# A new written order for the opening of a fused attention and routing kernel

## The chip, the cores and the metric

The kernel runs on one core of one Trainium2 chip. Its time is the device time of one execution in microseconds. Six executions of the kernel before gave a median of 715.14 us (713.99 to 716.82).

## What is computed

Duo attention feeds a mixture of experts whose routing is Sinkhorn-balanced. There are 4 batches, 8 heads, 768 positions and 64 values per head; heads with `is_retrieval` see all earlier positions, the others see the first 4 positions and the last 64.

```python
scores = q @ k.T / sqrt(64);  scores = where(mask, scores, -1e9)
a = exp(scores - max);  a /= a.sum(-1);  x = a @ v       # x: 3072 tokens x 512
logits = x @ w_gate;  P = exp(logits - logits.max())     # 8 experts
for _ in range(8):
    P /= P.sum(1, keepdims=True);  P /= P.sum(0, keepdims=True);  P *= N / E
out = sum over e of P[:, e:e+1] * (relu(x @ w1[e]) @ w2[e])   # 512 -> 1024 -> 512
```

## The kernel before

**Units, rounds and tasks.** Attention is cut into 24 units `(b, g, u)`: batch, a block of 256 queries, and half of the heads (two pairs `a` of two heads). For block `g` a pair has `g + 1` chunks of keys; each pair and chunk is a task, and two tasks make a round, of which there are 48. Rounds 0 and 1 are units 0 and 1 (first block), rounds 2 and 3 unit 2, rounds 4 and 5 unit 3 (second block); from round 6 on come the third block and the other batches.

**A unit's steps.** `emit_prep` transposes the keys and queries of a unit with 16 small products on PE into one bank of PSUM and has DVE copy them (L245) to `kT`. `scores(n)` emits the products of a round (L426) and, when it meets a unit, the loads of a batch-block three further on, on POOL's queue; it hands back two closures for each task, the exp on ACT (L435) and the masking on DVE (L444, L447), which `soften` calls. `sum_later` notes that a pair's chunks are complete, and `finish_sums` runs its products with v (L270), then the normalization (a reciprocal L283 and a multiplication L284 on DVE). All sums share one PSUM bank, tag "pv". `turn` transposes the normalized pairs of a unit on PE (L298), and ACT copies them to `xT` (L301). After the second half of the heads, `turn` also adds to the list `fillers` the steps of expert 0 for these 256 tokens: four layer-1 steps (L336, relu by DVE at L343) and two layer-2 steps (L350, copied out by ACT at L354). `fill(n)` spends them, counting a layer-1 step as one unit and a layer-2 step as two; `spend` is called after each round from 6 on and holds the units left to a line that runs from 96 down to 24 by round 47.

**v and the far keys.** For batch 0, v arrives in pairs of rows and is placed by `place_v(g)`: four products of a quarter of the array into a two-bank tile and one evacuation by ACT (L119). `farf` holds, for each head, which far keys count; `make_far_all` (L209, L212) spells it out to `farx` on ACT in three parts, and `emit_vfar` (L254) multiplies v with it on DVE. `make_masks` (L216) makes the four mask tiles, and `make_keep` their pattern.

**Order.** PE, DVE and ACT keep the order in which the opening is written, from the first spare products to the end of round 5 (L494 to L542). The loop over rounds 6 to 47 is outside of that block: there the framework's planner sets the order, by priority and by what it believes ready, and may place an instruction ahead into the opening's gaps. POOL's first loads are in written order (L370 to L394), its later ones are planned. PSUM has two double banks with tag "sc" (scores, and v in the kernel before), three single banks with tag "mo" (transposes, turns, fillers, spare products) and the "pv" bank. `warm(n)` issues n spare products of 512 columns, `keep_warm` at L260, whose results are never read.

**After attention** come 8 Sinkhorn iterations with the last 24 filler units between them, and then experts 1 to 7, with PE busy throughout.

Of the kernel before, what the change touches and what calls it, by code (L numbers as in the profile page):

```python
# [10 lines left out]
F32 = mybir.dt.float32  # L11
F16 = mybir.dt.float16
U32 = mybir.dt.uint32
AF = mybir.ActivationFunctionType
# [18 lines left out]
def kernel(  # L33
# [13 lines left out]
    nc = tc.nc  # L47
    B, H, S, D = q.shape
# [10 lines left out]
    DV = D + 2  # L59
# [12 lines left out]
    psA = attn.enter_context(tc.tile_pool(name="psA", bufs=1, space=bass.MemoryType.PSUM))  # L72
# [22 lines left out]
    def v_tile(b):  # L95
        if b not in vts:
            vts[b] = ap.tile([128, H, NC, DV], F16, tag="v16", name=f"v16_{b}")
            nc.vector.memset(vts[b][:, :, :, D:DV], 1.0)
        return vts[b]
# [8 lines left out]
        return raw  # L108

    def place_v(g):  # L110
        t = psA.tile([128, 2, 512], F32, tag="sc", bufs=2, name=f"vp_{g}")
        for n in range(2):
            rows = slice(64 * n, 64 * n + 64)
            for c in range(2):
                nc.tensor.matmul(
                    out=t[64 * c:64 * c + 64, n, :].rearrange("p (h d) -> p h d", h=H),
                    lhsT=ident16[rows, rows], rhs=vraw[g][rows, :, c, :], start=True, stop=True,
                )
        nc.scalar.activation(  # L119
            out=v_tile(0)[:, :, 2 * g:2 * g + 2, 0:D].rearrange("p h n d -> p n h d"),  # L120
            in_=t.rearrange("p n (h d) -> p n h d", h=H), func=AF.Copy, bias=0.0, scale=1.0,
        )

    def load_v_heads(b, h0, h1):
        for o in range(2):
# [30 lines left out]
    def round_first(h0):  # L156
# [9 lines left out]
        out=ret_u,  # L166
        in_=is_retrieval.bitcast(U32).unsqueeze(0).broadcast_to([128, 2 * H]),
# [19 lines left out]
        out=retf, in_=ret_u.rearrange("p (e two) -> p e two", two=2)[:, :, 0]  # L187
# [7 lines left out]
    farf = cp.tile([128, H, 2], F16, tag="farf")  # L195
    farx = cp.tile([128, H, 3, DV], F16, tag="farx")
# [7 lines left out]
                                    scalar2=None, op0=ALU.mult)  # L204
        nc.vector.tensor_copy(out=keep[:, 512:640], in_=keep[:, 256:384])

    def make_far_all():
        for n in range(2):
            nc.scalar.activation(  # L209
                out=farx[:, :, n], in_=farf[:, :, n].unsqueeze(2).broadcast_to([128, H, DV]),  # L210
                func=AF.Copy, bias=0.0, scale=1.0)
        nc.scalar.activation(out=farx[:, :, 2], in_=farx[:, :, 1], func=AF.Copy, bias=0.0, scale=1.0)  # L212

    def make_masks(js):
        for h in [2 * j + hh for j in js for hh in range(2)]:
            nc.vector.tensor_scalar(  # L216
                out=masks[h // 2][:, h % 2, :], in0=keep, scalar1=over[:, h:h + 1],
                scalar2=None, op0=ALU.is_gt,
            )

    def make_far():
        for i in range(2):
            nc.scalar.activation(out=farf[:, :, i], in_=retf, func=AF.Copy, bias=0.0, scale=1.0)
        for rows in sinks:
            nc.vector.memset(farf[rows, :, 0], 1.0)

    wg16 = constp.tile([128, 4, E], F16, tag="wg16")

# [3 lines left out]
    def emit_prep(b, g, u):  # L232
        tr = psA.tile([128, 512], F32, tag="mo", bufs=3, name=f"tr_{b}_{g}_{u}").bitcast(F16)
        for i, src in enumerate(kq[b, g]):
            for a in range(2):
                for c in range(2):
                    for hh in range(2):
                        nc.tensor.transpose(
                            out=tr[64 * hh:64 * hh + 64, ts(4 * i + 2 * a + c, 128)],
                            in_=src[:, 4 * u + 2 * a + hh, c, :], identity=ident16,  # L240
                        )
        t = ap.tile([128, 2, 2, 256], F16, tag=f"kT{u}{g}", bufs=1 + (g == 0),
                    name=f"kT_{b}_{g}_{u}")
        kTs[b, g, u], qTs[b, g, u] = t[:, 0], t[:, 1]
        nc.vector.tensor_copy(  # L245
            out=t.rearrange("r i a (n c p) -> r (i a) c n p", c=2, p=64),
            in_=tr.rearrange("r (i c n p) -> r i c n p", i=4, c=2, p=64),
        )

    def emit_vfar(b, g):  # L250
        if b not in vfs:
            vfs[b] = ap.tile([128, H, 4, DV], F16, tag="vf", bufs=1, name=f"vf_{b}")
        n = 2 * g - 2
        nc.vector.tensor_tensor(out=vfs[b][:, :, n:n + 2, :], in0=vts[b][:, :, n:n + 2, :],  # L254
                                in1=farx[:, :, g - 1:g + 1, :], op=ALU.mult)
# [35 lines left out]
    def turn():  # L291
        while turns:
            b, g, u = turns.pop(0)
            xn = xns.pop((b, g, u))
            xt = psA.tile([128, 512], F32, tag="mo", bufs=3, name=f"xt_{b}_{g}_{u}").bitcast(F16)
            for a in range(2):
                for sb in range(2):
                    nc.tensor.transpose(out=xt[:, ts(2 * a + sb, 128)], in_=xn[:, a, sb],  # L298
                                        identity=ident16)
            c0 = b * S + 256 * g  # L300
            nc.scalar.activation(  # L301
                out=xT[u][:, :, c0:c0 + 256], in_=xt[:, 0:512].rearrange("p (a c) -> p a c", a=2),
                func=AF.Copy, bias=0.0, scale=1.0)
            if u == 1:
                one, two = first_steps(b, g)
                at = 4 if (b, g) == (0, 1) else len(fillers)
                fillers[at:at] = one
                fillers.extend(two)

# [51 lines left out]
    fillers = []  # L361
# [8 lines left out]
    with tc.manual_schedule(engines={mybir.EngineType.Pool}):  # L370
        nc.gpsimd.affine_select(
            out=ident16, in_=ident16, compare_op=ALU.is_equal, fill=0.0,
            base=0, pattern=[[-1, 128]], channel_multiplier=1,
        )
        for o in range(2):
# [3 lines left out]
                out=f4, in_=f4, compare_op=ALU.is_ge, fill=0.0,  # L379
# [4 lines left out]
                out=w4, in_=w4, compare_op=ALU.is_ge, fill=0.0,  # L384
# [12 lines left out]
    PTs, sums, preps = {}, [], []  # L397
# [55 lines left out]
    left = [12 * 8]  # L453

    def fill(n):
        while n > 0 and fillers:
            done = fillers.pop(0)()
            n -= done
            left[0] -= done

    def finish_sums(between=None):
        for i, ((gen, scale), key) in enumerate([(sums_of[key], key) for key in sums_of]):
            if i and between:
                between()
            while run(gen, 1):
                pass
            del sums_of[key]
            scale[0]()

    rounds = len(tasks) // 2  # L470
    weights = [0] * 6 + [1] * (rounds - 6)

    def spend(n):
        fill(left[0] - (96 - 72 * sum(weights[:n + 1]) // sum(weights)))

    def sum_later(n):
        for i, a, ci in tasks[2 * n:2 * n + 2]:
            b, g, u = units[i]
            if ci == g:
                scale = []  # L480
                sums_of[i, a] = gen_pv(b, g, u, a, PTs.pop((i, a)), scale), scale

    def scores(n):
        return [emit_scores(*t) for t in tasks[2 * n:2 * n + 2]]

    def soften(pairs, which=(0, 1)):
        for pair in pairs:
            for w in which:
                pair[w]()

    def warm(n):
        keep_warm(ident16, kTs[units[0]].rearrange("p a s -> p (a s)"), n)

    engines = {mybir.EngineType.PE, mybir.EngineType.DVE, mybir.EngineType.Activation}  # L494
    with tc.manual_schedule(engines=engines):
        keep_warm(blank[:, 0:128], blank, 9)
        make_far()
        make_keep()
        round_first(0)
        emit_prep(*units[0])  # L500
        round_first(4)
        r0 = scores(0)
        soften(r0, (0,))
        warm(3)
        make_masks((0, 1))
        emit_prep(*preps.pop())
        warm(2)
        place_v(0)
        r1 = scores(1)
        soften(r0, (1,))  # L510
        soften(r1, (0,))
        sum_later(0)
        warm(6)
        make_masks((2, 3))
        soften(r1, (1,))
        finish_sums(lambda: emit_prep(*preps.pop()))
        warm(4)
        sum_later(1)
        r2 = scores(2)
        soften(r2, (0,))  # L520
        turn()
        make_far_all()
        soften(r2, (1,))
        finish_sums(lambda: emit_prep(*preps.pop()))
        sum_later(2)
        emit_vfar(0, 1)
        warm(2)
        soften(scores(3))
        place_v(1)
        turn()  # L530
        finish_sums()
        sum_later(3)
        warm(2)
        soften(scores(4))
        turn()
        finish_sums()
        sum_later(4)
        soften(scores(5))
        turn()
        finish_sums()  # L540
        sum_later(5)
        emit_prep(*preps.pop())  # L542
    for n in range(6, rounds):
        soften(scores(n))
        if n == 7:
# [19 lines left out]
    for it in range(8):  # L565
# [3 lines left out]
            out=Pne, in0=Pne, in1=rr.unsqueeze(2).broadcast_to([128, NB, E]), op=ALU.mult  # L569
# [281 lines left out]
```

## Time and profile before

| | us |
|---|---|
| median of six executions | 715.14 |
| the profiled execution | 715.48 |
| its span, first to last instruction | 713.7 |
| PE busy in the span | 691.3 |
| DVE, ACT, POOL busy | 571.3, 416.6, 151.5 |
| round 6's scores begin | 34.12 |
| Sinkhorn and the experts, from about | 180 |

In the profile, PE is the matmul engine and PEld its weight loads; DVE, ACT and POOL are the vector, scalar and GpSimd engines. A row of the timeline names engine, line of the kernel, operation, what is written and read, and how often; brackets give the idle time before it and what ended that. Names are shortened: `PT_1_0_0` is the weights of block 1, heads 0, pair 0; `sc_0_1` are the scores of pair 0, chunk 1; `tr`, `xt`, `pv`, `vp` and `l` are the banks of transposes, turns, sums, v's placement and fillers. The granted clock is PE's, as a share of full speed.

### The profile page before, as it was taken

What the parts mean: (1) busy time and instruction counts of PE and PEld (TensorE: products, weight loads), DVE (VectorE), ACT (ScalarE), POOL (GpSimd) and SP (SyncE); (2) the same over time, 40 slices, a digit from 0 to 9 for tenths busy, and PEclk for the clock granted to TensorE, in tenths of its full rate; (3) what the DMA queues carried; (4) which work ended last, traced back from release to release, by engine and by line L of the source; (5) the groups of instructions that cost most, each with busy time, mean ns of one, the idle gap of its engine ahead of it and who ended that gap; (6) DMA issues with size and microseconds to landing.
All of it is one profiled execution on the core that took longest, in us unless ns stands there. A gap on an engine that the chain in (4) does not pass through costs nothing.

```text
span 713.7 us, 17084 instructions
## 1 busy us (share of the span) xinstructions
PE 691.3 (97%) x6944; PEld 572.1 (80%) x6944; DVE 571.3 (80%) x1158; ACT 416.6 (58%) x776; POOL 151.5 (21%) x183
## 2 busy tenths in 40 slices
PE   7799999999999999999999999999999999999995
PEld 3566666666578888888888888888888888888884
DVE  6567575766789997988788878888898888877887
ACT  4677767675696555555555555555555555555550
POOL 7404040000011212122221222131212312121210
PEclk9899999999999999999999999999999999999999
DMA  9999393000632459435943495349543964245774
GB/s 178 179 177 105 31 106 31 2 2 1 107 57 46 75 93 147 74 61 89 160 78 57 71 160 90 57 72 151 92 73 61 143 109 75 52 79 109 147 158 125
DMA packets 84223, 65.61 MB, mean 92 GB/s; under 512 B 48304, under 2 KB 64688, under 8 KB 84144
## 3 DMA queue, kind: packets, MB, share of 16 engines
q0 software_dynamic: 74976, 57.17, 56.7%
q1 hardware_dynamic: 7536, 6.30, 3.7%
q8 instruction: 54, 0.88, 0.5%
q10 hardware_dynamic: 1632, 1.05, 0.5%
q14 instruction: 25, 0.20, 0.1%
HBM read 52.45 MB, written 6.29 MB: 82 GB/s over the span
## 4 chain that ended last, share of the span: by engine, by line
PE 68%; DVE 1%; issue 0%; ACT 0%; DVEq 0%
PE l1y L671 20%; PE l2y L739 19%; PE l2w L739 10%; PE l1w L671 10%; PE l2z L739 5%; PE l1z L671 5%; DVE acc_84 L756 1%; DVE S_7_5_10658 L609 0%; DVE S_7_5_10661 L609 0%; DVE S_7_5_10660 L609 0%; DVE acc_83 L756 0%; ACT R_3720 L680 0%; DVEq L846 0%; ACT add L753 0%; DVE S_7_5_10659 L609 0%
## 5 line engine op out<-in xcount | busy, mean ns | idle before, releaser
L753 ACT ACTIVATE add<-l2w,Pne 128x256 f32<-128x256 f32 x80 | 33.6, 473 | 66.1 <-PE l2w L739 64.2
L753 ACT ACTIVATE add<-l2y,Pne 128x256 f32<-128x256 f32 x80 | 33.7, 474 | 10.5 <-PE l2y L739 10.5
L336 PEld LDWEIGHTS <-w_0_126 128*128 128x128 f16 x384 | 35.6, 98 | 4.4 <-issue 0.6
L753 ACT ACTIVATE add<-l2z,Pne 128x256 f32<-128x256 f32 x80 | 33.6, 472 | 8.7 <-PE l2z L739 8.7
L761 POOL DMA_DIRECT2D acc_79<-add x21 | 17.7, 844 | 78.9 <-ACT add L753 57.8
L761 POOL DMA_DIRECT2D acc_82<-add x21 | 17.8, 847 | 68.0 <-ACT add L753 68.0
L761 POOL DMA_DIRECT2D acc_81<-add x21 | 17.7, 844 | 68.0 <-ACT add L753 68.0
L761 POOL DMA_DIRECT2D acc_80<-add x21 | 17.7, 845 | 67.9 <-ACT add L753 67.9
L761 POOL DMA_DIRECT2D acc_83<-add x18 | 15.1, 841 | 54.6 <-ACT add L753 46.8
L761 POOL DMA_DIRECT2D acc_84<-add x18 | 15.4, 854 | 43.8 <-ACT add L753 43.3
L756 DVE SCALAR_TENSOR_TENSOR acc_79<-l2y,Pne,acc_79 128x256 f32<-128x256 f32 x42 | 18.3, 477 | 7.2 <-PE l2y L739 7.1
L756 DVE SCALAR_TENSOR_TENSOR acc_83<-l2y,Pne,acc_83 128x256 f32<-128x256 f32 x44 | 19.1, 477 | 3.2 <-PE l2y L739 3.2
L756 DVE SCALAR_TENSOR_TENSOR acc_82<-l2y,Pne,acc_82 128x256 f32<-128x256 f32 x42 | 18.3, 476 | 4.1 <-PE l2y L739 4.1
L756 DVE SCALAR_TENSOR_TENSOR acc_80<-l2y,Pne,acc_80 128x256 f32<-128x256 f32 x42 | 18.3, 476 | 4.1 <-PE l2y L739 4.1
L756 DVE SCALAR_TENSOR_TENSOR acc_81<-l2y,Pne,acc_81 128x256 f32<-128x256 f32 x42 | 18.3, 476 | 4.0 <-PE l2y L739 4.0
L756 DVE SCALAR_TENSOR_TENSOR acc_84<-l2y,Pne,acc_84 128x256 f32<-128x256 f32 x36 | 15.7, 476 | 7.1 <-PE l2y L739 7.1
L671 PEld LDWEIGHTS <-S_5_6890 128*128 128x128 f16 x192 | 18.8, 98 | 2.2
L671 PEld LDWEIGHTS <-S_4_5856 128*128 128x128 f16 x192 | 18.8, 98 | 2.2
L671 PEld LDWEIGHTS <-S_2_3752 128*128 128x128 f16 x192 | 18.8, 98 | 2.2
L671 PEld LDWEIGHTS <-S_7_8958 128*128 128x128 f16 x192 | 18.8, 98 | 2.2
L671 PEld LDWEIGHTS <-S_3_4822 128*128 128x128 f16 x192 | 18.8, 98 | 2.2
L671 PEld LDWEIGHTS <-S_6_7924 128*128 128x128 f16 x192 | 18.8, 98 | 2.2
(2575 smaller groups left out, 2269.5 us busy)
## 6 DMA issues: line engine op xcount, KB each, us to landing
acc_79<-add POOLq DMA_DIRECT2D x21, 256.0 KB, 3.7
acc_80<-add POOLq DMA_DIRECT2D x21, 256.0 KB, 3.3
acc_81<-add POOLq DMA_DIRECT2D x21, 256.0 KB, 3.3
acc_82<-add POOLq DMA_DIRECT2D x21, 256.0 KB, 3.3
acc_83<-add POOLq DMA_DIRECT2D x18, 256.0 KB, 3.4
acc_84<-add POOLq DMA_DIRECT2D x18, 256.0 KB, 9.9
w_0_126<-in_moe_w_dram POOLq DMA_DIRECT2D x1, 1024.0 KB, 11.4
w_0_133<-in_moe_w_dram POOLq DMA_DIRECT2D x1, 1024.0 KB, 18.3
```

The source lines that it names most:

```text
L336: nc.tensor.matmul(out=l1[:, ts(fb % 2, 256)], lhsT=w1[:, dc, ts(fb, 128)], rhs=xT[dc // 2][:, dc % 2, c0:c0 + 256], start=(dc == 0), stop ...
L671: nc.tensor.matmul(out=banks[g, bank][:, f, :], lhsT=lefts1[e][k - 1][:, dc, ts(2 * g + f, 128)], rhs=rights1[c][k - 1][:, dc, :], start=( ...
L739: nc.tensor.matmul(out=banks[bank][q], lhsT=lefts2[e, c][k - 1][:, q, f, :], rhs=rights2[e][k - 1][:, f, :], start=(first and (final or q ...
L753: nc.scalar.activation(out=t[:, q, :], in_=banks[bank][q], func=AF.Copy, bias=0.0, scale=w)
L756: nc.vector.scalar_tensor_tensor(out=dst, in0=banks[bank][q], scalar=w, in1=dst, op0=ALU.mult, op1=ALU.add,)
L761: nc.gpsimd.dma_start(out=acc[c][:, i, n, :, :], in_=t, accum_op=ALU.add)
```

## The change

Four things change together. The opening's order is rewritten: unit 1's transposes are ahead of the spare products, unit 2's come before the first sum, round 2's scores stand between the two sums of unit 0, `turn` and some normalizations stand elsewhere among the masks, and the spare products in it go from nineteen to seven (the nine at the start stay). v is placed through two single "mo" banks with an evacuation each, where it took one two-bank "sc" tile. Two of the three parts of `farx` are spelled out at the start, in `make_far`, and the third after unit 1's turn. And four layer-1 filler units are spent in rounds 3 to 5, with `spend` running from 92 to 24 and the place where the second block's fillers go in counted from the end of the list.

```diff
     def place_v(g):
-        t = psA.tile([128, 2, 512], F32, tag="sc", bufs=2, name=f"vp_{g}")
         for n in range(2):
+            t = psA.tile([128, 512], F32, tag="mo", bufs=3, name=f"vp_{g}_{n}")
             rows = slice(64 * n, 64 * n + 64)
...
-        nc.scalar.activation(
-            out=v_tile(0)[:, :, 2 * g:2 * g + 2, 0:D].rearrange("p h n d -> p n h d"),
-            in_=t.rearrange("p n (h d) -> p n h d", h=H), func=AF.Copy, bias=0.0, scale=1.0,
-        )
+            nc.scalar.activation(
+                out=v_tile(0)[:, :, 2 * g + n, 0:D], in_=t.rearrange("p (h d) -> p h d", h=H),
+                func=AF.Copy, bias=0.0, scale=1.0,
+            )
...
+    def spell_far(n, src):
+        nc.scalar.activation(out=farx[:, :, n], in_=src, func=AF.Copy, bias=0.0, scale=1.0)
...
+        for i in (1, 0):
+            spell_far(i, farf[:, :, i].unsqueeze(2).broadcast_to([128, H, DV]))
...
-                at = 4 if (b, g) == (0, 1) else len(fillers)
+                at = len(fillers) - 2 * ((b, g) == (0, 1))
...
-    weights = [0] * 6 + [1] * (rounds - 6)
-
     def spend(n):
-        fill(left[0] - (96 - 72 * sum(weights[:n + 1]) // sum(weights)))
+        fill(left[0] - (92 - 68 * (n - 5) // (rounds - 6)))
...
         r0 = scores(0)
         soften(r0, (0,))
-        warm(3)
         make_masks((0, 1))
         emit_prep(*preps.pop())
+        warm(3)
+        r1 = scores(1)
+        soften(r1[:1], (0,))
+        place_v(0)
+        soften(r0, (1,))
+        sum_later(0)
+        soften(r1[1:], (0,))
+        make_masks((2, 3))
+        emit_prep(*preps.pop())
         warm(2)
-        place_v(0)
-        r1 = scores(1)
-        soften(r0, (1,))
-        soften(r1, (0,))
-        sum_later(0)
-        warm(6)
-        make_masks((2, 3))
+        r2 = []
+        finish_sums(lambda: r2.extend(scores(2)))
         soften(r1, (1,))
+        soften(r2, (0,))
+        warm(2)
+        turn()
+        sum_later(1)
+        emit_vfar(0, 1)
         finish_sums(lambda: emit_prep(*preps.pop()))
-        warm(4)
-        sum_later(1)
-        r2 = scores(2)
-        soften(r2, (0,))
+        place_v(1)
+        soften(r2, (1,))
+        sum_later(2)
+        r3 = scores(3)
+        soften(r3, (0,))
         turn()
-        make_far_all()
-        soften(r2, (1,))
-        finish_sums(lambda: emit_prep(*preps.pop()))
-        sum_later(2)
-        emit_vfar(0, 1)
-        warm(2)
-        soften(scores(3))
-        place_v(1)
-        turn()
+        spell_far(2, farx[:, :, 1])
         finish_sums()
+        soften(r3, (1,))
         sum_later(3)
-        warm(2)
+        fill(1)
         soften(scores(4))
-        turn()
         finish_sums()
         sum_later(4)
+        fill(1)
+        emit_prep(*preps.pop())
         soften(scores(5))
         turn()
         finish_sums()
         sum_later(5)
-        emit_prep(*preps.pop())
+        fill(2)
```

More of the change, by code (lines that the diff above doesn't have):

```diff
@@ L115, in place_v @@
                 nc.tensor.matmul(
-                    out=t[64 * c:64 * c + 64, n, :].rearrange("p (h d) -> p h d", h=H),
+                    out=t[64 * c:64 * c + 64, :].rearrange("p (h d) -> p h d", h=H),
                     lhsT=ident16[rows, rows], rhs=vraw[g][rows, :, c, :], start=True, stop=True,
                 )
-        nc.scalar.activation(
-            out=v_tile(0)[:, :, 2 * g:2 * g + 2, 0:D].rearrange("p h n d -> p n h d"),
-            in_=t.rearrange("p n (h d) -> p n h d", h=H), func=AF.Copy, bias=0.0, scale=1.0,
-        )
+            nc.scalar.activation(
+                out=v_tile(0)[:, :, 2 * g + n, 0:D], in_=t.rearrange("p (h d) -> p h d", h=H),
+                func=AF.Copy, bias=0.0, scale=1.0,
+            )
     def load_v_heads(b, h0, h1):
@@ L205, in make_keep @@
         nc.vector.tensor_copy(out=keep[:, 512:640], in_=keep[:, 256:384])
[L207 to L212, printed above, removed]
+    def spell_far(n, src):
+        nc.scalar.activation(out=farx[:, :, n], in_=src, func=AF.Copy, bias=0.0, scale=1.0)
     def make_masks(js):
```

## The prediction

> **What bounds it now.** I read the page first: who is busy, and when.
>
> ```profile
> span 713.7 us, 17084 instructions
> PE 691.3 (97%) x6944; PEld 572.1 (80%) x6944; DVE 571.3 (80%) x1158; ACT 416.6 (58%) x776; POOL 151.5 (21%) x183
> PE   7799999999999999999999999999999999999995
> ```
>
> PE is the bound nearly everywhere; only the first two slices (35.7 us) show 7. So the change can win only the opening's PE idle time and PE work that need not exist. The same by stretches (us from the span's start; busy us and instruction counts of PE, PEld, DVE, ACT, POOL; granted clock; DMA share; GB/s):
>
> ```profile
> 18.75:27.40 8.65, 5.83 (x75) 3.46 (x75) 5.26 (x14) 7.15 (x10) 3.73 (x4) 0.82 1.53 196
> 27.40:36.05 8.65, 7.33 (x111) 5.56 (x112) 4.72 (x12) 5.17 (x7) 4.73 (x6) 0.79 2.43 162
> 36.05:60.00 23.95, 22.63 (x311) 14.96 (x312) 16.40 (x38) 16.34 (x23) 5.09 (x6) 1.00 1.36 159
> 60.00:195.00 135.00, 131.50 (x1700) 87.72 (x1699) 90.21 (x231) 93.06 (x136) 15.21 (x17) 1.00 0.47 44
> ```
>
> After 36 us PE idles 3% with ACT at 69%, so time saved before 36 us is kept. Before it the chain goes through ACT and DVE. The waits between 7 and 36 us (who, for whom: us, times, longest):
>
> ```profile
> ACT PT_2_0_0_564 L435 <- PE sc_0_0_565 L426: 2.9, 1, 2.9
> ACT PT_1_0_0_342 L435 <- PE sc_0_0_343 L426: 2.9, 1, 2.9
> ACT v_0_247 L119 <- PE vp_242 L115: 2.8, 1, 2.8
> PE pv_0_1_1_396 L270 <- DVE xn_0_1_373 L284: 1.7, 1, 1.7
> POOL v_1_336 L126 <- DMA w_0_126<-in_moe_w_dram: 3.7, 1, 3.7
> ```
>
> ACT three times sits nearly 3 us for products that PE could have made earlier. In order of time around the 1.7 us wait (start, us, engine, line):
>
> ```profile
> 17.82 1.02 PE L260 MATMUL warm<-kT_0_0_187,ident_93 128*128 128x512 f16 x4
> 20.13 0.81 ACT L435 ACTIVATE PT_1_0_0_342<-sc_0_1_348 128x768 f16<-128x768 f32 x1
> 20.97 0.56 DVE L447 TENSOR_TENSOR PT_1_0_0_342<-PT_1_0_0_342,mask_106 128x768 f16<-128x768 f16 x1 [0.41 <-ACT PT_1_0_0_342 L435]
> 21.44 0.17 DVE L283 RECIPROCAL rc_0_1_0_374<-pv_0_1_0_366 128x4 f32<-128x4 f32 x1
> 22.14 0.36 PE L270 MATMUL pv_0_1_1_396<-v_0_247,PT_0_1_1_256 128*128 128x65 f16 x6 [1.72 <-DVE xn_0_1_373 L284]
> ```
>
> The normalization of unit 1's first sum (21.44) is written behind unit 2's mask (20.97), which waits for an exp (20.13); the next sum needs the same PSUM bank and waits too.
>
> **What is removed.** Nineteen spare products after the first nine become seven. Six took 1.31 us (15.23 to 16.54), 0.22 each; three took 1.39 (9.84 to 11.23), 0.46 each. Twelve fewer are 2.6 us at the fast pace, but most fill waits: no separate credit, only through the walk below.
>
> **What is added or lengthened.** Placing v in halves: two 128x512 evacuations at 0.60 (the xT row's size and time) for one of 1.02, +0.18 each; three placements, 0.5 us of ACT. The two 0.6 us spellings of farx (L209, 1.19 together) move into ACT's idle 5.02 to 6.45, behind the sink memsets that end before 5.18 (DVE's next start): done by about 6.4, so the first rounding, at 6.45, isn't late; without that cover they would cost 1.2. The third (0.64) follows xT's copy. Behind it is only round 4's exp, which PE doesn't feed before 25; cost 0.
>
> **The walk.** I take each instruction's duration from its row, in the new written order on each engine. PE: 16 transposes 0.5 (1.0 slow), scores of a first-block pair 0.2 each (0.37 slow), of a second-block pair 0.2, sums 0.3 and 0.45, turn 0.25. ACT: exps 0.81 and 1.02. DVE: key copy 0.69, two masks 1.05 (first block) or 0.85, mask making 2.1 or 1.6 for four, normalization 0.6, vfar 0.7, relu 0.69. Unit 1's transposes now follow the scores directly: PE 9.84 to 10.8; DVE has finished mask making at 11.0 and copies to 11.7 (13.02 before). Three spares end at 12.1, round 1's scores at 12.8, v's products at 13.3, ACT's first exp at 13.45 and v's copies at 14.65, the second exp at 15.45. Unit 2's transposes end by 14.3 and its key copy 15.2; sum 15.1 to 15.4, round 2's scores until 15.85 (19.2 before), exps done 17.65; second sum 16.5, xn 17.2, masks of round 1 18.3, vfar 19.0. Unit 1's sums: 17.8 to 18.1 and, after the normalization at 19.6, 19.65 to 19.95. Round 3's scores end at 20.6, but ACT has v's second placement until 21.55, so the exps end 23.35. Unit 2's first sum is at 21.8 to 22.25; xT follows at 24.0. **The new stall:** the first filler (l1 reads both xT) holds PE from 22.25 to 24.05; round 4's scores are queued behind it, and ACT waits for them until 25.2. Then filler 24.95, scores 25.35, sum 25.85, filler 26.75, transposes 27.25, scores 27.65; turn waits for the normalization behind round 4's masks (28.2), sum 28.95, two fillers 30.7. Round 6's scores thus begin at 30.7 with four layer-1 steps done; before, 34.12 with none.
>
> To compare like with like: the planner, which orders all from round 6 on, had put unit 5's transposes and part of a sum ahead. At 36.05 the old kernel had done round 6's scores, those transposes, that sum and one step. After needs 0.4+0.5+0.45 more: 32.05, with four steps. A step is eight matmuls, 0.87 us (47.15 to 48.02). Lead: 4.0+3x0.87=6.6.
>
> **The clock** takes some back. The first columns as above; the clock is before the DMA share:
>
> ```profile
> 17.50:20.90 3.40, 2.79 (x44) 1.73 (x44) 1.60 (x6) 1.69 (x3) 1.67 (x2) 1.00 1.75 182
> 20.90:24.35 3.45, 1.28 (x16) 0.71 (x17) 2.81 (x8) 3.29 (x7) 1.18 (x2) 0.99 1.47 198
> 24.35:27.75 3.40, 3.25 (x30) 1.78 (x31) 2.07 (x5) 2.18 (x3) 0.89 (x1) 0.51 1.48 197
> 27.75:31.20 3.45, 2.13 (x39) 1.41 (x34) 1.57 (x5) 3.25 (x5) 1.78 (x2) 0.98 1.99 174
> 31.20:34.60 3.40, 3.40 (x57) 2.92 (x56) 2.55 (x5) 0.59 (x2) 2.17 (x4) 0.52 2.80 153
> ```
>
> A stretch with 1.28 or 2.13 busy is followed by one at half clock, one with 2.79 isn't. The Trainium skill (TensorE: Matmul & The Clock Gate, "HAM oscillation") asks only that no idle gap exceed about 3.4 us; my longest is 1.8, so by the rule no stretch goes slow and the lead is 6.6. The trace contradicts it: its longest gap there was 1.72, and it went slow twice. By the row, my 0.8 us of busy time in 20.9 to 24.35 makes the next stretch slow; redoing it with doubled matmuls ends round 5 at 31.6 instead of 30.7, lead 5.7. I take that. My 14.1 to 17.5 and 17.5 to 20.9 hold about 1.9 each, between 1.28 and 2.79: slow would cost 0.5 to 1 each, and if the first stretch starts late, more (below).
>
> **Moved steps and their DMAs.** Round 2's scores also issue the next batch's key, query and v loads, and a 0.14 memset. POOL isn't in written order there; it waits for earlier transfers to land (the 3.7 us above, until 18.73), so nothing loads sooner or collides. Landings (issue plus time to landing): layer-1 weights 18.5, third keys and queries 19.9 and 22.6, layer-2 weights 28.9. They are wanted at 24, 26.75 and after 31: slack 2.3 us at least. If the layer-2 weights were 3 us late, PE would lose up to 1.
>
> **Later.** The new count spreads 68 units over rounds 6 to 47 where 72 were. With 3% idle I let 85% of three steps' 2.6 us survive: 2.2. Bounds: all, 2.6; nothing, 0, if waits replace fillers. v's third placement now takes two of three "mo" banks, which fillers use: between 0 and 1 us, I take 0.5 with its longer copies. Sum: 5.7-2.6+2.2-0.5=4.8. Profiled execution: 715.48 (713.7 span and 1.78 around it), hence 710.7; the median of the runs is 0.34 lower, hence **710.4**.
>
> **Rivals.** (a) Gain mostly lost: more stretches slow, or the fillers merely swap for waits. Taking 1 for each of the two doubtful stretches and letting no later filler gain survive leaves 0.6 to 3: 713. For it: seven spares against nineteen; against: PE's 97%. (b) The planner fills my 1.8 us hole with unit 5's transposes, as it hoisted them before, and no stretch slows: lead 6.6 or more, 708.5. (c) **Slower**: with spares gone, PE never leaves half speed in the opening. The walk with all PE durations doubled begins round 6 at 36.7 and reaches the common point at 39.2, three steps ahead, against 36.05+2.6=38.65 for the old one: +0.55. Each further slow stretch of 3.4 us in the saturated part costs 1.7; two make 717 to 719. It decides if the clock is still half past about 36 us. For it: PE ran the first 14 us at the slow pace despite nine spares, and a stretch of about 75% activity (7.3 to 10.7) did not lift it. Against: 10.7 to 14.1 is still nearly solid, and four fillers are dense. (d) No effect: PE idle in the opening only hides the DMA. Against: no PE wait there is on a transfer; time 715.
>
> **Numbers.** Mine 0.58 (own range 708.3 to 712.5), (a) 0.19, (b) 0.08, (c) 0.12, (d) 0.03. Range 707.5 to 714.9: it takes in (b) and (a) and leaves out the slower case. A measurement of this kernel can tell about 0.2% (1.4 us). Faster: mine, (b), and three quarters of (a), 0.80; same: (d) and part of (a), 0.07; slower 0.13.
>
> **What would show it.** Unit 1's key copy ends near 11.7; round 2's scores near 15.6; ACT's two 2.9 us waits shrink under 1; PE's 1.7 us wait goes; a new wait of l1 for xT near 23; round 6's scores near 31.6, four l1 steps before them; one half-clock stretch around 24 to 28, none at 31 to 35. Wrong if PE shows half clock over 14 to 24 us, if a filler waits for weights, or if PE idles more than 5% past 36 us.

## The result, and the profile after

The changed kernel took 709.06 us (median of ten executions, 707.93 to 710.13) beside 715.62 us for the kernel before on the same chip. The ratio is 0.9909, with a 95% interval of 0.9899 to 0.9919: 6.5 us faster, where the prediction took off 4.7. The profiled execution took 708.54 us.

The page of the changed kernel: span, engines, and PE in 40 slices.

```profile
span 706.8 us, 17061 instructions
PE 685.7 (97%) x6932; PEld 568.7 (80%) x6932; DVE 569.1 (81%) x1157; ACT 418.0 (59%) x780; POOL 151.6 (21%) x183
PE   7899999999999999999999999999999999999996
```

PE has twelve matmuls fewer, which are the spare products, and is busy 5.6 us less in a span that is 6.9 us shorter. The only slice besides the last that still shows less than 8 is the first; the second rose from 7 to 8. By stretches of the same kernel (start and end; sum, then busy us and counts of PE, PEld, DVE, ACT, POOL; granted clock; DMA share; GB/s):

```profile
18.75:27.40 8.65, 6.70 (x111) 4.77 (x112) 6.40 (x17) 6.29 (x9) 3.68 (x4) 1.00 1.54 195
27.40:36.05 8.65, 8.19 (x114) 5.35 (x111) 5.15 (x13) 6.43 (x11) 4.83 (x6) 1.00 2.07 172
36.05:60.00 23.95, 23.10 (x357) 15.98 (x354) 16.45 (x42) 17.58 (x27) 7.80 (x9) 1.00 1.81 182
60.00:195.00 135.00, 131.36 (x1646) 87.70 (x1644) 91.41 (x231) 96.77 (x144) 12.48 (x14) 1.00 0.44 43
```

From 18.75 to 36.05 PE is busy 14.89 us where it was 13.16, and makes 225 matmuls where it made 186. The granted clock is full in both stretches; it was 0.82 and 0.79. The waits of the changed kernel between 7 and 36 us (who, for whom: us, times, longest):

```profile
ACT v_0_256 L119 <- PE vp_1_395 L115: 1.9, 1, 1.9
ACT PT_0_1_0_240 L433 <- PE sc_0_0_241 L424: 1.6, 1, 1.6
PE l_446 L334 <- ACT xT_77 L299: 1.6, 1, 1.6
ACT PT_2_0_0_584 L433 <- PE sc_0_0_585 L424: 1.1, 1, 1.1
PE pv_0_1_1_381 L268 <- DVE xn_0_1_358 L282: 0.7, 1, 0.7
```

ACT's three waits of nearly 3 us are gone; the longest that remains is 1.9. PE's wait for the normalization fell from 1.7 to 0.7. The third row is the new stall, a filler that waits for `xT`. The same things in order of time (start, us, engine, line):

```profile
10.77 0.69 DVE L243 COPY kT_0_1_232<-tr_0_1_215 128x1024 f16<-128x1024 f16 x1
...
14.93 0.39 PE L424 MATMUL sc_0_0_315<-kT_1_0_287,kT_0_0_189 64*128 64x256 f16 x4
...
18.93 0.36 PE L268 MATMUL pv_0_1_1_381<-v_0_256,PT_0_1_1_246 128*128 128x65 f16 x6 [0.71 <-DVE xn_0_1_358 L282]
...
22.91 0.38 PE L334 MATMUL l_446<-xT_77,w_0_126 128*128 128x256 f16 x2 [1.59 <-ACT xT_77 L299]
...
29.45 0.39 PE L424 MATMUL sc_0_0_585<-kT_2_0_516,kT_0_0_189 64*128 64x256 f16 x4
...
30.81 0.35 PE L268 MATMUL pv_1_1_1_617<-v_0_256,PT_1_1_1_518 128*128 128x65 f16 x6
```

Unit 1's keys are copied by 11.46, round 2's scores start at 14.93, and round 6's at 29.45 where they started at 34.12. By 31.00, when a layer-2 step starts, round 6's scores, unit 5's transposes and unit 3's last sum are done, with four layer-1 steps. The old kernel was there at 36.05 with one step. So the lead is 5.05 us and three steps, 3 x 0.87 = 2.61: 7.66 us.

What PE did up to this common point tells what the lead consists of (columns as above; before, then after):

```profile
7.00:36.05 29.05, 23.07 (x279) 13.75 (x281) 19.11 (x48) 18.01 (x26) 15.58 (x19) 0.88 1.80 185
```

```profile
7.00:31.00 24.00, 19.34 (x292) 12.77 (x293) 19.87 (x50) 16.95 (x26) 12.77 (x16) 0.93 1.59 192
```

PE was idle for 5.98 us and now is for 4.66, which is 1.3 of the 7.66. The spare products behind the first nine took 6.6 us of PE's busy time and now take 2.8: 3.8. The other 2.5 is real products that take less time for the same work. The old kernel ran them at half clock from 24.25 to 27.67 and from 31.09 to 34.50 by the record, and at half pace before about 14; the changed kernel has none after 12.4, and its repeat below none after 14.4. In that repeat the idle time is 4.07 us, 1.9 less than before.

The lead can be read again where the experts begin. Their first product (PE's timeline), first before, then after:

```profile
188.56 0.59 PE L652 MATMUL l1b<-xT_76,w_1_2410 128*128 128x512 f16 x2
```

```profile
180.71 0.59 PE L651 MATMUL l1b<-xT_76,w_1_2402 128*128 128x512 f16 x2
```

7.85 us: nothing that was won in the opening is lost in the rounds. From there to the end of the span the old kernel took 525.1 us and the new one 526.1. All the profiles of this case lie between 525.1 and 526.6 in that stretch, so this 0.95 is spread of the experts, which the change doesn't touch. It leaves 6.9 us in the span.

### The profile page after: what moved, and what is told of

Read it like the earlier page. It is cut to its first block, busy times and chain, and to the rows that moved or that the text cites. A ratio compares the mean times of both kernels' runs of the same rounds, so it can differ in the third digit from the quotient of the medians.

```text
span 706.8 us, 17061 instructions
## 1 busy us (share of the span) xinstructions
PE 685.7 (97%) x6932; PEld 568.7 (80%) x6932; DVE 569.1 (81%) x1157; ACT 418.0 (59%) x780; POOL 151.6 (21%) x183
## 3 DMA queue, kind: packets, MB, share of 16 engines
q10 hardware_dynamic: 1632, 1.05, 0.5%
## 5 line engine op out<-in xcount | busy, mean ns | idle before, releaser
L760 POOL DMA_DIRECT2D acc_79<-add x21 | 17.7, 844 | 78.6 <-ACT add L752 60.4
L760 POOL DMA_DIRECT2D acc_81<-add x21 | 17.7, 844 | 68.9 <-ACT add L752 67.1
```

What stands on the lines that cost most here:

```text
L760: nc.gpsimd.dma_start(out=acc[c][:, i, n, :, :], in_=t, accum_op=ALU.add)
```

## The experiments

Three theories were put to the chip. The **order theory**: the written order shortens the opening, and the parts of it named in the prediction carry that. The **filler theory**: what counts is that layer-1 steps fill PE's gaps early. The **clock theory**, the prediction's rival (c) turned into a question: spare products decide when PE leaves half speed, so their number matters. Notes behind a # in the edits are not in the kernels. Beside the times the profiles give two lengths: the opening, from the start of the first scores to the start of round 6's, and the start of the experts. The changed kernel has 20.5 us (8.95 to 29.45) and 180.71; the kernel before has 25.0 (9.08 to 34.12) and 188.56. Both are read from one execution of each run, which in a_nofill, a_undo3, a_oldv and a_maskfirst was the longest of four. The start of the first scores varies by 0.8 us between the runs, which the opening leaves out and the start of the experts does not.

### The order without the early fillers, and the fillers without the order

a_nofill is the changed kernel with the old count and place of fillers:

```diff
-                at = len(fillers) - 2 * ((b, g) == (0, 1))
+                at = 4 if (b, g) == (0, 1) else len(fillers)
...
-        fill(left[0] - (92 - 68 * (n - 5) // (rounds - 6)))
+        fill(left[0] - (96 - 72 * max(0, n - 5) // (rounds - 6)))
...
-        fill(1)     # round 3
...
-        fill(1)     # round 4
...
-        fill(2)     # round 5
```

> The changed kernel with its new order and few spares, but without the four filler steps in rounds 3 to 5 (the count runs from 96 to 24 over rounds 6 to 47 again, and the second block's steps go in at index 4). Order theory: round 4's scores no longer stand behind a filler that waits for xT, so round 6 begins about 3 us earlier than the changed kernel's 29.45, near 26.5, but 3.5 us of steps are still to be done: about 0.5 us worse than the changed kernel, 5.5 to 6 us better than before, near 709.7. Filler theory (the gain comes from steps put into gaps): half of the gain goes, near 712.3.

709.33 us, ratio 0.9919 (0.9904 to 0.9934). Opening 17.9 us, experts at 182.11.

b_fill is the kernel before with the four fillers in rounds 3 to 5 and the new count and place (not shown again):

```diff
         sum_later(3)
         warm(2)
+        fill(1)
...
         sum_later(4)
+        fill(1)
...
         emit_prep(*preps.pop())
+        fill(2)
```

> The kernel before, its order and nineteen spares kept, with the four filler steps spent in rounds 3 to 5 and the new count. Order theory: the steps meet only some 1.3 us of PE waits between 27.4 and 36, and the activity may keep the clock up over 31 to 35: 1 to 2.5 us better than before, near 713.7. Filler theory: 3 to 4 us better, near 712. If each step merely delays round 6: no change.

713.80 us, ratio 0.9980 (0.9967 to 0.9992). Opening 25.9 us, experts at 186.86.

The filler theory falls. The order with its fewer spares gives 6.3 us without any filler (5.8 by the ratio) of the 6.5, and the fillers alone 1.8 (1.4 by the ratio). In the new order the fillers lengthen the opening by 2.6 us and save 3.5 us of steps later, which leaves 0.9. The experts start 1.4 us later without them, of which 0.5 is a later start of the first scores; by the ratios the fillers are worth 0.7, and the intervals overlap. The gains alone sum to 7.2 by the ratios, where the change has 6.5. That would fit idle time which both close, but the difference is within the intervals.

### The spare products

b_fewspare is the kernel before with seven spares after the first nine, as many as the changed kernel has:

```diff
-        warm(6)
+        warm(2)
...
-        warm(4)
...
         emit_vfar(0, 1)
-        warm(2)
...
         sum_later(3)
-        warm(2)
```

> The kernel before with seven spares in place of nineteen after the first nine (three, two, two, none after), everything else as it was. Order theory: the spares lie in waits, so nothing is won, and a further slow stretch may cost up to 1.7 us: 715.4, 714.7 to 717. Spare theory (the spares themselves are the cost): 2.6 us better, 713.0.

713.52 us, ratio 0.9970 (0.9959 to 0.9981). Opening 23.1 us, experts at 186.46. A miss: the order theory gave nothing to this edit, and it won 2.1 us. PE's timeline between the spares and the first sum, in the kernel before and then in this one:

```profile
15.23 1.47 PE L260 MATMUL warm<-kT_0_0_187,ident_93 128*128 128x512 f16 x6
16.54 0.35 PE L270 MATMUL pv_0_0_0_284<-v_0_247,PT_0_0_0_195 128*128 128x65 f16 x6
```

```profile
15.46 1.04 PE L260 MATMUL warm<-kT,ident 128*128 128x512 f16 x2
16.29 0.54 PE L270 MATMUL pv<-v,PT 128*128 128x65 f16 x6
```

In the kernel before v had been placed at 14.90, and the first sum waited behind six spares. Four more, from 17.82, stood ahead of round 2's scores, for which ACT idled 2.9 us. Taking these away won little there, since PE was slow: the first sum came 0.25 us earlier and round 2's scores 0.16 (18.61 where it was 18.77). Round 3's scores came 0.45 earlier, and round 4's 1.08 (26.32 where it was 27.40), where the two spares from 26.43, 0.97 us at half clock, stood straight ahead of them. Round 6's came 1.88 earlier; after 28.6 the record shows no half clock in this kernel, while the old one had it from 31.09. So spares were on the path, but how much of the last 0.8 us is the clock's isn't separated. Until 28 us the clock was against this kernel: by its windows (columns as above), PE ran at 0.61 and then 0.50 of full speed.

```profile
9.00:24.00 15.00, 11.43 (x119) 6.14 (x120) 11.25 (x29) 9.31 (x14) 7.96 (x9) 0.61 1.52 195
24.00:28.00 4.00, 3.72 (x44) 2.61 (x43) 2.07 (x5) 3.32 (x6) 0.89 (x1) 0.50 1.48 197
```

a_manyspare is the changed kernel with twelve spares more, eight at places where PE was expected to wait anyway and four ahead of the first sum, which they were expected to delay:

```diff
-        warm(2)     # ahead of unit 0's sums
+        warm(6)
...
-        warm(2)     # after round 2's first exp
+        warm(6)
...
-        finish_sums(lambda: emit_prep(*preps.pop()))
+        finish_sums(lambda: (emit_prep(*preps.pop()), warm(2)))
...
         sum_later(3)
+        warm(2)
         fill(1)
```

> The changed kernel with nineteen spares again, the twelve added ones at its waits (four ahead of the first sum, four ahead of unit 0's turn, two behind unit 1's second transposes' round, two ahead of the first filler). Order theory: some fall into waits of 0.7 and 1.6 us, four delay the first sum by 0.9: 0.5 to 1.2 us worse than the changed kernel, near 710. Spare theory: 2.6 us worse, 711.7. If spares are needed for the clock: as the changed kernel or better, 709.

709.14 us, ratio 0.9915 (0.9900 to 0.9929). Opening 21.5 us, experts at 182.15. By the times no cost of twelve spares shows in the new order (the intervals leave room for about 1 us either way), and their absence wins 2.1 in the old one. By the profile's opening they cost about 1.

a_nospare is the changed kernel with the seven taken out:

```diff
-        warm(3)
...
-        warm(2)     # ahead of unit 0's sums
...
-        warm(2)     # after round 2's first exp
```

> The changed kernel without any spare product after the first nine. Clock theory (the slower rival of the prediction: without spares PE stays at half speed through the opening): slow pace past 14 us or further slow stretches up to 36 us, 1.7 us each, 1.5 to 5 us worse than the changed kernel, 711 to 714. Order theory (the real products keep PE active enough, and the seven spares lie in waits or delay round 1's scores by some tenths): within 0.7 of the changed kernel.

709.27 us, ratio 0.9926 (0.9912 to 0.9940), beside 709.05 us and 0.9923 (0.9909 to 0.9936) for the changed kernel on the same chip. Opening 20.9 us, experts at 181.04. The windows of a_nospare:

```profile
10.50:14.00 3.50, 2.71 (x38) 1.51 (x33) 3.38 (x10) 2.33 (x5) 2.64 (x4) 0.50 1.59 196
14.00:17.50 3.50, 2.56 (x29) 1.58 (x28) 2.63 (x8) 2.73 (x5) 0.88 (x1) 0.50 1.12 211
17.50:20.90 3.40, 3.27 (x42) 1.98 (x40) 3.20 (x9) 1.21 (x3) 0.95 (x1) 0.50 1.76 181
20.90:24.35 3.45, 2.62 (x32) 2.09 (x33) 1.85 (x5) 2.84 (x5) 1.83 (x2) 0.82 1.46 201
```

PE is at half speed from 8.7 until 22.1 us, which is what rival (c) feared, and it costs nothing that can be measured: round 6's scores start at 29.80 and in the changed kernel beside it, which has half clock from 7.7 to 14.4, at 29.81. While PE is slow it is busy longer, but it still waits in three of the four windows, so other engines pace part of the work. The seven spares, 2.8 us of PE, are gone too and may make up for some of the slow clock. The clock theory falls for the stretch up to 22 us: doing without spares loses nothing that shows.

### The three named parts of the order

a_undo3 is the changed kernel with the three things undone that the walk rests on: unit 1's keys behind the spares again, v through one "sc" double bank with one evacuation, and round 2's scores behind both sums:

```diff
-        make_masks((0, 1))
-        emit_prep(*preps.pop())
         warm(3)
+        make_masks((0, 1))
+        emit_prep(*preps.pop())
...
-        r2 = []
-        finish_sums(lambda: r2.extend(scores(2)))
+        finish_sums()
         soften(r1, (1,))
+        r2 = scores(2)
```

with the old `place_v`.

> The changed kernel with the three things undone that its name lists: three spares ahead of unit 1's transposes again, v placed through one double scores bank, round 2's scores behind both of unit 0's sums. Spares (seven), masks, turns, farx and fillers stay as changed. Theory that the whole chain's shift makes the gain: unit 1's key copy 0.7 us later in effect, the first sum 0.4 to 0.8 later for the single v evacuation ahead of round 1's second exp, round 2's exps 0.5 later but with slack: 1.0 to 1.8 us worse than the changed kernel, near 710.5. Theory that these three are the gain: 4 us or more worse, 713 or above.

711.97 us, ratio 0.9962 (0.9946 to 0.9977), between the two expectations: 2.8 to 3.8 us worse than the changed kernel, and 2.7 better than the one before. Opening 24.4 us, experts at 185.20. Its timeline:

```profile
13.18 0.82 PE L424 MATMUL sc<-kT 64*128 64x256 f16 x8 [0.79 <-DVE kT L243]
14.58 0.64 PE L115 MATMUL vp<-acc,ident 64*64 64x512 f16 x4 [0.58 <-ACT PT L433]
...
19.56 1.04 PE L258 MATMUL warm<-kT,ident 128*128 128x512 f16 x2
...
24.48 0.51 PE L424 MATMUL sc<-kT 64*128 64x256 f16 x4 [0.59 <-ACT v L119]
```

PE waits for the keys (0.79), v's placement waits for the first exp to empty its double bank (0.58), and later the scores wait for v's evacuation to empty one (0.59): three waits that the changed kernel doesn't have, 2.0 us together. But PE also kept the half pace here until 27.8, as shown at the end, where the changed kernel reached full pace by 12.4 and its repeat by 14.4. So the loss is not shown to be that of the three moves alone; the slow pace is a rival that this run leaves standing.

a_r2late undoes only the last of the three:

```diff
-        r2 = []
-        finish_sums(lambda: r2.extend(scores(2)))
+        finish_sums()
         soften(r1, (1,))
+        r2 = scores(2)
```

> The changed kernel with round 2's scores behind both sums of unit 0, nothing else. Exps of round 2 end about 18.2 instead of 17.1, and their masks are wanted at 19.9 only: no loss, 709.1, 708.6 to 709.6. Rival (ACT is the chain there, any late score costs in full): 1 us worse, 710.1.

708.50 us, ratio 0.9916 (0.9901 to 0.9931). Opening 20.4 us, experts at 180.87. Round 2's scores between the sums show no worth by themselves. ACT does wait for them, 1.37 us where it waited 0.27, but the masks behind these exps follow only near 20, and the wait is gone by then.

a_oldv undoes only v's placement (the removed lines of `place_v` in the change, put back).

> The changed kernel with v placed through one double scores bank and one evacuation again, nothing else. Round 2's first scores and the first sum wait for the whole placement and round 2's second scores for round 1's second exp: 0.4 to 0.8 us worse than the changed kernel, near 709.6. If it only saves 0.5 us of ACT: no change or 0.3 better.

710.45 us, ratio 0.9932 (0.9914 to 0.9950). Opening 22.1 us, experts at 183.09. PE's timeline shows two waits of the kind that a_undo3 has:

```profile
13.98 0.64 PE L115 MATMUL vp<-acc,ident 64*64 64x512 f16 x4 [0.58 <-ACT PT L433]
...
22.84 0.34 PE L424 MATMUL sc<-kT 64*128 64x256 f16 x4 [0.81 <-ACT v L119]
```

0.58 + 0.81 = 1.4 us of waits, and 0.6 to 1.6 us of time by the ratio to the two measurements of the changed kernel (0.9909 and 0.9923), whose intervals it overlaps. Its matmuls also kept the half pace until some 17.7 us, and this run doesn't separate that from the waits. The keys' place alone wasn't run.

### PE's wait for the normalization

In the old order a mask stood ahead of unit 1's normalization. a_maskfirst puts it back there:

```diff
         emit_vfar(0, 1)
+        soften(r2, (1,))
         finish_sums(lambda: emit_prep(*preps.pop()))
         place_v(1)
-        soften(r2, (1,))
```

> The changed kernel with round 2's masks written ahead of unit 1's sums again, as in the kernel before; nothing else. On DVE 0.85 us of masks stand ahead of the first normalization, the second sum, v's second placement (written behind it on PE) and round 3's scores move by as much: 0.7 to 1.0 us worse than the changed kernel, near 709.9. If the 1.6 us wait of the first filler swallows it: no loss, 709.1.

709.70 us, ratio 0.9934 (0.9919 to 0.9949). Opening 22.6 us, experts at 183.55. The wait is 1.39 us where it was 0.71 (timeline):

```profile
20.60 0.36 PE L268 MATMUL pv<-v,PT 128*128 128x65 f16 x6 [1.39 <-DVE xn L282]
```

The ratio is 0.8 to 1.8 us worse than that of the changed kernel, but the intervals meet or overlap. The 0.7 us of wait accounts for part; the rest of the 2 us that the opening grew lies in the half-clock stretch that followed (windows shown below). That stretch is seen in one execution of 711.25 us; the other three took 709.06 to 709.96.

### Two attempts to do better

The new stall is a filler that waits for `xT`. a_fill_later puts round 4's scores ahead of it:

```diff
         sum_later(3)
-        fill(1)
         soften(scores(4))
+        fill(1)
```

> The changed kernel with the first filler step behind round 4's scores instead of ahead of them. The 1.6 us wait for xT then no longer holds up round 4's scores (near 22.4 instead of 23.7), but the exps behind them find ACT with xT's copy and farx's last part until 23.4 where they began at 24.1: 0.5 to 0.7 us better than the changed kernel. If that wait is swallowed later by PE's later idle time: no change.

708.67 us, ratio 0.9914 (0.9901 to 0.9928). Opening 20.8 us, experts at 181.01. PE's gap is used, and the end of the opening doesn't move. The 0.4 us by the medians is within the intervals.

a_best adds to this that the third spelling of `farx` goes ahead of `xT`'s copy of unit 1, into ACT's 1.9 us wait:

```diff
         turn()      # unit 0
+        spell_far(2, farx[:, :, 1])
...
         turn()      # unit 1
-        spell_far(2, farx[:, :, 1])
```

> As the run with the first filler behind round 4's scores, and farx's last part spelled out after unit 0's turn, where ACT has 1.9 us idle, instead of after unit 1's. Round 4's exps begin near 22.9 instead of 24.1: round 6 begins near 28.3 instead of 29.45, 1.0 to 1.3 us better than the changed kernel. If the rest of the opening is bound by the masks and normalizations on DVE: 0.5 or less.

708.19 us, ratio 0.9908 (0.9892 to 0.9923). Opening 19.7 us, the shortest with all fillers, and experts at 180.40. And the changed kernel once more, beside these:

> The changed kernel itself, beside the runs it is compared with: 0.991 of the kernel before, within 0.1%. A profile in which half-clock stretches fall elsewhere than in its first one would show that they differ from execution to execution.

709.05 us, ratio 0.9923 (0.9909 to 0.9936), opening 20.7 us, experts at 181.05. Its profile shows no half clock after 14.4, as the first one showed none after 12.4. a_best is 0.86 us better by the medians and 1.0 us by the opening, but the intervals overlap, so a gain isn't established by time.

## Why the prediction was right, and where its sizes were off

**The bound and the direction** held, though idle time is the smallest part of the win. Of the lead of 7.66 us at the common point 1.3 is less idle time, 3.8 fewer spares and 2.5 shorter real products. The prediction's bound named idle time and needless work; it left out that the old opening ran about 6.8 us at half clock after 24 us. The walk did reckon with it, without saying so, because it took nearly all products at full pace. That time won before 36 us is kept holds: the order with fewer spares gave 5.8 to 6.3 us. That PE idles 3% after 36 us holds only past 60; from 36 to 60 the old kernel idled 5.5% (22.63 busy of 23.95) and the new one 3.5%.

**The walk** named the right points: keys copied at 11.7 (measured 11.46), v's copies done at 14.65 (14.39), round 2's scores ending at 15.85 (started at 14.93), unit 1's second sum at 19.65 (18.93), the new stall's end at 24.05 (22.91). Without a slow stretch, round 6's scores were put at 30.7 and the common point at 32.05; they came at 29.45 and 31.00, about 1.05 early. The walk added rows end to end, and rows of one engine overlap. In the changed kernel:

```profile
9.46 0.81 ACT L433 ACTIVATE PT_0_0_0_197<-sc_0_0_198 128x768 f16<-128x768 f32 x1
10.16 0.81 ACT L433 ACTIVATE PT_0_0_1_203<-sc_1_0_204 128x768 f16<-128x768 f32 x1
...
13.31 0.59 ACT L119 ACTIVATE v_0_256<-vp_0_253 128x512 f16<-128x512 f32 x1
13.79 0.60 ACT L119 ACTIVATE v_0_256<-vp_1_259 128x512 f16<-128x512 f32 x1
```

The exps last 0.81 and start 0.70 apart; v's evacuations last 0.59 and start 0.48 apart. So v in halves costs 2 x 0.48 and not 2 x 0.60 where one of 1.02 stood, and the +0.18 for each placement was too much. About 0.1 us for each of the ten or so instructions in a row on ACT or DVE makes up the 1.05; that is worked out from the rows and not tested alone.

**The clock** was the step that failed most clearly. By the row of before, a stretch with little PE work would be followed by half clock, and 0.9 us was taken off for it. The rule of the Trainium skill (TensorE: Matmul & The Clock Gate, "HAM oscillation"), that no idle gap may exceed about 3.4 us, would have taken nothing off. The windows of the changed kernel:

```profile
20.90:24.35 3.45, 1.86 (x29) 1.23 (x27) 2.31 (x6) 2.74 (x5) 2.09 (x3) 1.00 1.46 201
24.35:27.75 3.40, 3.27 (x66) 2.54 (x62) 2.54 (x7) 2.66 (x4) 0.89 (x1) 1.00 1.48 196
```

1.86 us busy of 3.45, a gap of 1.59, and the next stretch stays at full clock: here the rule was right. But part of the reason is that the hole was smaller than the walk made it (1.86 busy, not 0.8). And the rule doesn't settle it either. a_maskfirst's windows:

```profile
17.00:20.45 3.45, 1.84 (x31) 1.04 (x27) 3.26 (x9) 1.68 (x3) 0.95 (x1) 1.00 1.62 187
20.45:23.85 3.40, 3.25 (x38) 2.25 (x39) 1.48 (x6) 2.50 (x4) 1.34 (x2) 0.60 1.58 194
23.85:27.30 3.45, 2.77 (x24) 1.61 (x23) 2.39 (x5) 1.90 (x4) 1.38 (x2) 0.50 1.35 203
```

The same busy time, a longest gap of 1.39 us, and half clock follows, from 21.13 to 27.96. Measured over the 3.4 us that end where the clock falls, PE is busy 1.74 in a_maskfirst and 2.08 at the second fall in the kernel before, at 31.09; the changed kernel's emptiest 3.4 us from 17 us on hold 1.76, and its clock stays full. Neither the gap nor the busy time tells these apart; what decides stays open.

**The spares**: "most fill waits" was wrong as a statement on the old order, for b_fewspare won 2.1 us with nothing else changed. It cost the sum nothing, because the walk, which the credit was to come through, left the twelve out. In the new order twelve more cost about 1 us of the opening and nothing that the times show (a_manyspare).

**farx at no cost** held: its two spellings run on ACT from 5.11 to 6.28, and the first rounding then waits for its data until 6.54. So did the **DMAs**: no product waited for a weight, and the first layer-2 step, at 31.00, directly follows the sum.

**Later**: 2.2 of three steps' 2.6 us were to survive, and 0.5 was taken off for the "mo" banks. The lead went from 7.66 at the common point to 7.85 at the experts. All of it survived, and neither term shows: +0.9.

So the sum at the experts' start was 4.8, and the trace shows 7.85: 1.05 from the walk, 0.9 from the clock, 0.9 from the later rounds, and 0.2 that appears between the opening and the experts. Of that, 6.5 us is in the time. **Rival (a)**, gain mostly lost, fell with the last two of these. **Rival (b)** came nearest in time (708.5), though not by its mechanism: unit 5's transposes still come after round 6's scores, and the stall stayed. **Rival (c)** fell with a_nospare, **(d)** with the result.

**Of the expected signs**, the keys' copy, round 2's scores and the stall near 23 came. PE's wait for the normalization, which was to go, shrank from 1.7 to 0.7. ACT's wait for round 2's scores went to 0.3 and the one for round 6's to 1.1, a little over the 1 that was given; instead there are waits of 1.6 for round 1's scores and 1.9 for v. Round 6's scores came two microseconds earlier than the 31.6 that was given, and no stretch at half clock showed.

What stays open: how the 6.3 us of the order divides, and how much of it is the half clock that went. The named three are worth 2.8 to 3.8 us together, with a slow pace in it, v's banks 0.6 to 1.6 of it, round 2's scores none that shows. The spares are worth 2.1 in the old order and about 1 or less in the new. The rest of the moves (masks, turns, v's second placement, unit 2's transposes) weren't run alone.

## What to carry to other kernels

Walk a written order engine by engine and look for what each engine would be waiting on; time taken off the path of a stage where no engine is full is kept to the end, if a full engine follows. Not every wait lies on that path: ACT's grew by 1.1 us in a_r2late, and PE's 1.6 us was put to use in a_fill_later, and neither moved the end by anything that shows. Gains of such edits need not add up (here 6.3 for the order and 1.8 for the fillers stood beside 6.5 together), so measure them together and apart. Before a win is put down to idle time, split the busy time too: here 1.3 us of 7.66 was idle time, and the rest spares and slower products. Spare work that keeps an engine warm is worth checking for what stands behind it: here twelve of them, some straight ahead of awaited scores, cost 2.1 us in the old order, although PE ran at half speed until 28 us without them.

## What the runs showed of the hardware

A granted clock of 1.00 at the start of a profile is no evidence of full speed. In the windows of a_undo3 it reads:

```profile
15.80:19.20 3.40, 2.67 (x28) 1.56 (x26) 1.66 (x5) 1.19 (x2) 0.28 (x1) 1.00 1.42 194
19.20:22.60 3.40, 3.40 (x40) 2.28 (x36) 2.67 (x8) 2.30 (x3) 2.34 (x3) 1.00 1.74 187
```

while the two spares at 19.56, shown above, take 1.04 us together, as the two at 15.46 in b_fewspare do at a recorded 0.50 (8.25 to 18.25), and the products keep the half pace until some 27.8 us: a filler's eight take 1.75 us at 26.11 and 1.04 at 28.72. In the profile of before three spares took 1.39 us at 9.84 under a clock of 1.00, 0.46 each, and six took 1.31 at 15.23, 0.22 each. Until the record shows its first change, the products' own pace has to be read.

Half-clock stretches that began after 20 us lasted 3.4 us or twice that: 24.25 to 27.67 and 31.09 to 34.50 in the profile of before, 21.13 to 27.96 in a_maskfirst, 21.72 to 28.55 in b_fewspare.

PE at half speed for 13 us, with seven spares fewer, cost nothing that shows (a_nospare, 709.27 beside 709.05 us). In a_maskfirst half clock for 7 us went with an opening longer by 2 us where PE was busy 3.25 of 3.40.
